# Sigmoid attention followed by a GELU MLP on one core: another order of the first loads and of TensorE's work at the start, and a last output tile in three pieces with merged stores

## The chip, the cores and the metric

The kernel runs on one core of a Trainium2 chip. The metric is the device time of one execution in microseconds (us). The kernel before takes 391.43 us (median of 3 runs, 391.25 to 391.61).

## The reference, cut to what matters

```python
# q, k, v: batch 8, heads 12, S = 448, head size 64
scores = matmul(q, k.T) / sqrt(64) - log(S)
attn   = 1 / (1 + exp(-scores))                # sigmoid, no row sums
x      = matmul(attn, v), heads side by side   # 3584 x 768
h      = x @ w_in                              # 768 x 2048
g      = 0.5 * h * (1 + tanh(c * (h + 0.044715 * h**3)))   # GELU
out    = g @ w_out                             # 2048 x 768, float32
```

## The kernel before: the parts that the change and the argument touch

The program is made by a small scheduler in Python. It simulates the engines with estimated durations, picks the next operation for each engine, and then writes out one fixed order for each. On the chip every engine follows its order and waits on semaphores; if the first operation in line has to wait, everything behind it waits too (1.23 us of TensorE in the run warm_late below).

Four heads form a *group* (3 groups per batch, 24 in all). A group has 7 score tiles ("units"). Each unit needs q and k cast to bfloat16 and transposed; four matmuls give scores of 128x896; ScalarE turns them into attention weights; four *av* matmuls add them to x transposed (xT). In the first batch (units 0 to 20) ScalarE uses Sigmoid; later batches use Tanh, and VectorE finishes the work. Tanh lies in the same table set as GELU: the profile has only two table loads, at 2.32 and 26.81 us, and after the second Tanh and GELU alternate. The MLP's first product (`make_a`, w_in) needs a complete xT of a batch; the second (`make_b`, w_out) gives tiles of 128 rows.

```python
# first group: two column ranges of q and of k, one DMA each
CUTS = ((0, NJ // 2 + 1), (NJ // 2 + 1, NJ))
for x, (lo, hi) in enumerate(CUTS):
    ld[(0, x)] = plan.add(Op("ld%s0.%d" % (nm, x),
        "AQ" if (nm, x) in (("q", 0), ("k", 1)) else "SP",     # ScalarE's or SyncE's queue
        lambda e, ...: e.dma_start(d[:, :, lo * D:hi * D], ap[:, :, lo * D:hi * D]), ...))
# ... cut ...
# the GELU table, after the last sigmoid has ended
if n == SIG * NG * NJ - 1:
    plan.add(Op("warm2", "ACT", lambda e: e.activation(warm[:], warm[:], AF.Gelu_apprx_tanh), [tanh[n]], ...))
# ... cut ...
# one output tile: two halves of 384 columns; rows of two strips, 64 partitions each
def make_b(t_, half, t):
    # ... 16 matmuls of 128x384 into one PSUM bank, copy to ob ...
    if half == 1 or last:
        for x in range(2):
            b, j = two[x]
            dst = out[b * S:(b + 1) * S, lo:hi].rearrange("(r j) d -> r j d", j=NJ)[:, j, :]
            def fn(e, x=x, dst=dst):
                return e.dma_start(dst, ob[o][64 * x:64 * x + 64, lo:hi])   # 64 rows per DMA
            if last and half == 1 and x == 1:
                at_end.append((fn, ev))                # the very last one on ScalarE's queue
                continue
            sts.append(plan.add(Op("st%d.%d" % (t_, x), "SP", fn, ...)))
# ... cut ...
# TensorE's choice before the MLP may start (not mlp)
if can and left <= 1 and free_pairs(t) and banks >= (2 if av_open else 4):
    return make_qk(n, t)                   # next score tile
if m and not soon:
    return av_take(1, t)[0]                # next av
if trans_ready(t) and banks >= (1 if soon or not 0 < n < UB else 3):
    return make_trans(t)                   # transposes of a coming group
nxt = part_ready(t)                        # two matmuls of the MLP's first product, early
return make_part(*nxt, t) if nxt and (nxt[1] or banks >= HBANKS) else None
```

## Time and profile before

| what | number | view |
|---|---|---|
| TensorE in the chain of waits | 92% of the span of 390.2 us | chain |
| first / last sigmoid starts | 7.97 / 24.89 us | timeline of ScalarE |
| xT of the first batch complete | 27.64 us | timeline of VectorE |
| first matmul of the second product | 62.03 us | timeline of TensorE |
| last copy ends; last store lands | 387.35; 389.75 us | timeline, landings |

Of the page: the first line is the span, the second the busy time of each engine with its share, the third the chain of work that ended last, by engine. In the lines below, L726 and L764 are the MLP's two products, L592 the scores, L639 the av.

```profile
span 390.2 us, 7414 instructions
PE 382.1 (98%) x3173; PEld 200.1 (51%) x3173; DVE 134.1 (34%) x229; ACT 241.9 (62%) x380; POOL 50.1 (13%) x82
PE 92%; DMA 3%; POOL 2%; ACT 1%; issue 0%
```

TensorE bounds the kernel from about 30 us to the end. Only the two ends can be shortened without taking work away. The timeline of ScalarE at the start (start us, duration us, engine, line, operation, tiles, count):

```profile
7.97 17.83 ACT L603 ACTIVATE at<-ps 128x896 bf16<-128x896 f32 x21 [0.89 <-PE ps L592]
25.87 0.92 ACT L611 ACTIVATE th<-ps 128x896 f32<-128x896 f32 x1
26.81 1.28 ACT L607 ACT_TABLE_LOAD   x1
```

The 21 sigmoids are 20 steps of 0.797 us at best (15.94 us); from first to last start they took 16.92 us, so 0.97 us was lost in gaps. TensorE's timeline shows how: at 10.07 the transposes of k and of q stand together between two score tiles (L592). At the end of the batch the last av (26.07) stands behind one more score tile (25.86).

```profile
9.75 0.38 PE L592 MATMUL ps<-qT,kT 64*64 64x448 bf16 x4
10.07 0.56 PE L546 MATMUL ps<-ident,kb 128*128 128x128 bf16 x7
10.47 0.56 PE L546 MATMUL ps<-ident,qb 128*128 128x128 bf16 x7
10.95 0.38 PE L592 MATMUL ps<-qT,kT 64*64 64x448 bf16 x4
...
25.86 0.38 PE L592 MATMUL ps<-qT,kT 64*64 64x448 bf16 x4
26.07 0.36 PE L639 MATMUL ps<-at,vb 64*64 64x448 bf16 x4
```

The end: the copies of the last tile's halves, and the DMA issue on ScalarE's queue, in the timeline.

```profile
384.26 0.49 ACT L351 ACTIVATE ob<-ps 128x384 f32<-128x384 f32 x1 [2.11 <-PE ps L764]
386.86 0.49 ACT L351 ACTIVATE ob<-ps 128x384 f32<-128x384 f32 x1 [2.11 <-PE ps L764]
387.38 0.55 ACTq L798 DMA_DIRECT2D out_dram<-ob  x1
```

The DMA issues (count, KB each, median us from issue to landing): the last tile's four stores of 64 rows land in 2.1 to 2.4 us.

```profile
out_dram<-ob SPq DMA_DIRECT2D x3, 96.0 KB, 2.1
out_dram<-ob ACTq DMA_DIRECT2D x1, 96.0 KB, 2.4
```

### The profile page before, as it was taken

The numbers are of one execution on the slowest core, as the hardware profiler recorded it, in microseconds if no ns is written. First come the engines' busy times: TensorE is split into PE (matmuls) and PEld (weight loads), VectorE is DVE, ScalarE is ACT, GpSimd is POOL, SyncE is SP. The second block draws the span as 40 slices with busy tenths as digits, with TensorE's granted clock in tenths as the row PEclk, the third lists the DMA queues.
The fourth block names the chain that finished last, engine by engine and source line by source line (L and its number), as shares of the span: only waits on it lengthen the run. The fifth ranks groups of instructions, "written<-read, shape, count | busy, mean of one in ns | idle before, by whom it ended". The sixth has DMA issues, their size and how long they took to land.

```text
span 390.2 us, 7414 instructions
## 1 busy us (share of the span) xinstructions
PE 382.1 (98%) x3173; PEld 200.1 (51%) x3173; DVE 134.1 (34%) x229; ACT 241.9 (62%) x380; POOL 50.1 (13%) x82
## 2 busy tenths in 40 slices
PE   7889999999999999999999999999999999999996
PEld 4334445545554555555555555555454555555563
DVE  3347622146634547154334423444333200000000
ACT  4999963488768888577665757575757532333221
POOL 5992110011101101110110101110000000000000
PEclk9999999999999999999999999999999999999999
DMA  8999999847984969666657818747111011111133
GB/s 229 192 195 203 210 202 306 148 113 124 284 155 126 208 159 186 164 131 176 144 121 165 179 29 183 181 69 186 40 43 42 0 42 40 42 40 42 40 81 82
DMA packets 64033, 51.74 MB, mean 133 GB/s; under 512 B 36224, under 2 KB 60544, under 8 KB 64000
## 3 DMA queue, kind: packets, MB, share of 16 engines
q1 hardware_dynamic: 48576, 36.61, 39.0%
q0 software_dynamic: 14528, 13.64, 22.2%
q10 hardware_dynamic: 896, 1.02, 0.7%
q8 instruction: 25, 0.41, 0.4%
q14 instruction: 8, 0.07, 0.1%
HBM read 45.61 MB, written 11.01 MB: 145 GB/s over the span
## 4 chain that ended last, share of the span: by engine, by line
PE 92%; DMA 3%; POOL 2%; ACT 1%; issue 0%
PE ps L726 38%; PE ps L764 38%; PE ps L592 9%; PE ps L639 7%; DMA w_in<-in_moe_w_in_dram 2%; DMA kf<-in_k_dram 1%; POOL vb L478 1%; POOL vb L480 1%; PE ps L549 1%; POOL w_in L819 0%; ACT th L611 0%; POOL qb L450 0%; POOL kb L450 0%; ACT L607 0%; PE ps L702 0%
## 5 line engine op out<-in xcount | busy, mean ns | idle before, releaser
L726 PE MATMUL ps<-xT,w_in 128*128 128x448 bf16 x756 | 153.2, 353 | 0.0
L764 PE MATMUL ps<-w_out,gT 128*128 128x384 bf16 x896 | 153.1, 326 | 0.0
L615 DVE TENSOR_SCALAR at<-th 128x896 bf16<-128x896 f32 x147 | 91.7, 628 | 134.2 <-ACT th L611 134.0
L611 ACT ACTIVATE th<-ps 128x896 f32<-128x896 f32 x147 | 129.9, 930 | 0.7 <-PE ps L592 0.7
L764 PEld LDWEIGHTS ps<-w_out,gT 128*128 128x128 bf16 x896 | 86.6, 98 | 62.5 <-issue 2.9
L726 PEld LDWEIGHTS ps<-xT,w_in 128*128 128x128 bf16 x756 | 70.5, 98 | 74.9 <-issue 7.7
L740 ACT ACTIVATE gT<-ps 128x448 bf16<-128x448 f32 x128 | 71.2, 557 | 41.8 <-PE ps L726 41.7
L351 ACT ACTIVATE ob<-ps 128x384 f32<-128x384 f32 x56 | 27.5, 490 | 95.5 <-PE ps L764 95.5
L592 PE MATMUL ps<-qT,kT 64*64 64x448 bf16 x672 | 49.4, 360 | 2.3 <-ACT at L603 1.9
L478 POOL DMA_DIRECT2D vb<-in_v_dram x24 | 14.6, 608 | 211.9 <-PE ps L592 208.3
L639 PE MATMUL ps<-at,vb 64*64 64x448 bf16 x672 | 38.3, 350 | 0.0
L592 PEld LDWEIGHTS ps<-qT,kT 64*64 64x64 bf16 x672 | 15.2, 105 | 29.2 <-issue 14.5
L639 PEld LDWEIGHTS ps<-at,vb 64*64 64x64 bf16 x672 | 19.6, 107 | 11.4 <-issue 0.7
L352 DVE CAST xT<-ps 128x448 bf16<-128x448 f32 x26 | 15.8, 618 | 13.4 <-PE ps L639 13.4
L352 DVE CAST kb<-kf 128x896 bf16<-128x896 f32 (+2 forms) x21 | 12.7, 607 | 17.7 <-DMA kf<-in_k_dram 17.6
L603 ACT ACTIVATE at<-ps 128x896 bf16<-128x896 f32 x21 | 17.5, 934 | 1.2 <-PE ps L592 0.9
L480 POOL DMA_DIRECT2D vb<-in_v_dram x24 | 16.8, 699 | 0.2 <-issue 0.2
L352 DVE CAST qb<-qf 128x896 bf16<-128x896 f32 (+1 forms) x20 | 12.3, 614 | 10.8 <-DMA qf<-in_q_dram 10.8
L351 ACT ACTIVATE xT<-ps 128x448 bf16<-128x448 f32 x22 | 12.2, 563 | 1.9 <-PE ps L639 1.9
L819 POOL DMA_DIRECT2D w_in<-in_moe_w_in_dram x16 | 9.9, 655 | 0.0
L405 PE MATMUL ps<-gT,ident 128*128 128x256 bf16 x25 | 5.7, 392 | 2.0 <-POOL ident L359 1.5
L405 PEld LDWEIGHTS ps<-gT,ident 128*128 128x128 bf16 x25 | 3.3, 141 | 3.4 <-POOL ident L359 1.5
(29 smaller groups left out, 38.7 us busy)
## 6 DMA issues: line engine op xcount, KB each, us to landing
out_dram<-ob SPq DMA_DIRECT2D x54, 192.0 KB, 2.7
kf<-in_k_dram SPq DMA_DIRECT2D x19, 448.0 KB, 3.9
qf<-in_q_dram SPq DMA_DIRECT2D x18, 448.0 KB, 5.7
vb<-in_v_dram POOLq DMA_DIRECT2D x48, 112.0 KB, 5.8
w_in<-in_moe_w_in_dram POOLq DMA_DIRECT2D x16, 192.0 KB, 11.2
w_out<-in_moe_w_out_dram POOLq DMA_DIRECT2D x4, 768.0 KB, 23.1
kb<-in_k_dram POOLq DMA_DIRECT2D x4, 224.0 KB, 8.9
qb<-in_q_dram POOLq DMA_DIRECT2D x4, 224.0 KB, 9.6
```

The costliest lines, as they stand in the source:

```text
L351: return e.activation(o, i, AF.Copy)
L352: return e.tensor_copy(o, i)
L478: a = plan.add(Op("ldv%da" % g, "SWQ", lambda e, d=dst[0:64], ap=lo: e.dma_start(d, ap), deps, 610.0, 0.0, prio=order_v(g), sem="ldv%da" % ...
L480: c = plan.add(Op("ldv%db" % g, "SWQ", lambda e, d=dst[64:128], ap=hi: e.dma_start(d, ap), deps, 610.0, 0.0, prio=order_v(g), sem="ldv%db" ...
L592: r = mm(ps[64 * half:64 * half + 64, (x, y)[a], 0:S], kv[d, a, j, :], qv[d, a, :, :], start=True, stop=True)
L603: lambda e: e.activation(at[as_][:], both, AF.Sigmoid, bias=bias, scale=scale),
L611: lambda e: e.activation(th[ts][:], both, AF.Tanh, bias=0.5 * bias, scale=0.5 * scale),
L615: lambda e: e.tensor_scalar(at[as_][:], th[ts][:], 0.5, 0.5, op0=ALU.mult, op1=ALU.add),
L639: r = mm(ps[64 * c:64 * c + 64, banks[a], 0:S], vb[s][d, slot, j, :], at[as_][d, a, :], start=(j == 0), stop=(j == NJ - 1))
L726: r = mm(ps[:, bank, 0:S], w_in[:, kt, fc * 128:(fc + 1) * 128], xT[xb][:, kt, :], start=(kt == 0), stop=(kt == KT - 1))
L740: lambda e: e.activation(gT[:, fc, col:col + S], ps[:, bank, 0:S], AF.Gelu_apprx_tanh),
L764: r = mm(ps[:, bank, 0:EH], gT[:, fc, col:col + 128], w_out[:, fc, half * EH:(half + 1) * EH], start=(fc == 0), stop=(fc == FC - 1))
```

## The change

The intent: have the first scores earlier (q's second part over both load queues), keep ScalarE's sigmoids free of gaps (no transpose close to the next score tile, scores of the second batch held until xT is complete), load the GELU table right behind the sigmoids, and make the last copy and store short (three pieces of 384, 256 and 128 columns). The core of the diff:

```diff
+    QLATE = 1
+    HOLD = 200.0
@@ first loads: q's second part as two DMAs, one on each queue; k's second part moves to SyncE's queue
-                        ld[(0, x)] = plan.add(Op("ld%s0.%d" % (nm, x), "AQ" if (nm, x) in (("q", 0), ("k", 1)) else "SP", ...
+                        both = [plan.add(Op("ld%s0.%d.%d" % (nm, x, c), eng, ... d[:, c:c + w, lo * D:hi * D] ...))
+                                for (eng, c, w) in ((("SP", 0, 1), ("AQ", 1, 1)) if (nm, x) == ("q", 1) else
+                                                    (("AQ" if nm == "q" else "SP", 0, 2),))]
+                        ld[(0, x)] = All(both)
@@ GELU table
-                    plan.add(Op("warm2", "ACT", ..., [tanh[n]], 1500.0, 1500.0))
+                    other.append(plan.add(Op("warm2", "ACT", ..., [op], 1500.0, 1500.0, prio=(1, n))))
...                                       # and each tanh waits for `other` in the plan
@@ last tile
+        def pieces(t_):
+            if t_ < NT - 1:
+                return [(0, EH), (EH, DM)]
+            return [(0, EH), (EH, DM - 128), (DM - 128, DM)]
...
+                if last and not end:
+                    b, j = two[0]
+                    dst = out[b * S:(b + 1) * S, lo:hi].rearrange("(r j) d -> j r d", j=NJ)[j:j + 2]
+                    sts.append(plan.add(Op("st%d" % t_, "SP", lambda e: e.dma_start(dst, ob[o][:, lo:hi]), [ev], ...
+                    return op
@@ TensorE's choice before the MLP
-                if can and left <= 1 and free_pairs(t) and banks >= (2 if av_open else 4):
+                if can and left <= 1 and (n < UB + 2 - QLATE or (0, KT - 1) in evac) and free_pairs(t) and ...
-                if m and not soon:
+                if m and not soon and (state["av"] < NG or m == NJ):
                     return av_take(1, t)[0]
+                ends = [tanh[x].end for x in range(max(0, n - 4), n) if ... tanh[x].end > t]
+                if 0 < n < UB and can and ends and min(ends) < t + HOLD:
+                    return None
-                return make_part(*nxt, t) if nxt and (nxt[1] or banks >= HBANKS) else None
+                return make_part(*nxt, t) if nxt and (nxt[1] or banks >= (HBANKS if n <= UB + 1 - QLATE else 1)) else None
```

The first two pieces of the last tile: their two stores of 64 rows have become one DMA of 128 rows, `j r d`.

More of the change, by code (lines that the diff above doesn't have):

```diff
@@ L417, in bass_sigmoid_attention__then__act_gelu_tanh_kernel @@
         trans = []
+        other = []
         EARLY = ("v0 q2 v1 v2 q3 v3 w0 w1 q4 v4 w2 q5 v5 w3 o0 o1 o2 o3").split()
@@ L455, in load_qk @@
                     for x, (lo, hi) in enumerate(CUTS):
-                        ld[(0, x)] = plan.add(Op("ld%s0.%d" % (nm, x), "AQ" if (nm, x) in (("q", 0), ("k", 1)) else "SP",
-                                                 lambda e, ap=ap, d=dst[0], lo=lo, hi=hi: e.dma_start(
-                                                     d[:, :, lo * D:hi * D], ap[:, :, lo * D:hi * D]),
-                                                 [], 460.0, 0.0, prio=(2, x - 2),
-                                                 sem="ld%s0.%d" % (nm, x), pkt=(16, 89.0 * (hi - lo) / NJ)))
+                        both = [plan.add(Op("ld%s0.%d.%d" % (nm, x, c), eng,
+                                            lambda e, ap=ap, d=dst[0], lo=lo, hi=hi, c=c: e.dma_start(
+                                                d[:, c:c + w, lo * D:hi * D], ap[:, c:c + w, lo * D:hi * D]),
+                                            [], 490.0, 0.0, prio=(2, -3 if x == 0 else -2 if nm == "q" else -1),
+                                            sem="ld%s0.%d.%d" % (nm, x, c), pkt=(8 * w, 89.0 * (hi - lo) / NJ)))
+                                for (eng, c, w) in ((("SP", 0, 1), ("AQ", 1, 1)) if (nm, x) == ("q", 1) else
+                                                    (("AQ" if nm == "q" else "SP", 0, 2),))]
+                        ld[(0, x)] = All(both)
                     ld[g] = ld[(0, 1)]
@@ L474, in load_v @@
             dst = vb[s][:].rearrange("p s j d -> p s (j d)")
-            deps = later(av, g - NVB) + ([ld_k[(0, 0)]] if g == 0 else [])
+            deps = later(av, g - NVB) + (ld_k[(0, 0)].ops if g == 0 else [])
             if g >= PE_TR * NG:
@@ L606, in make_qk @@
                 if n == SIG * NG * NJ - 1:
-                    plan.add(Op("warm2", "ACT", lambda e: e.activation(warm[:], warm[:], AF.Gelu_apprx_tanh),
-                                [tanh[n]], 1500.0, 1500.0))
+                    other.append(plan.add(Op("warm2", "ACT",
+                                             lambda e: e.activation(warm[:], warm[:], AF.Gelu_apprx_tanh),
+                                             [op], 1500.0, 1500.0, prio=(1, n))))
             else:
@@ L612, in make_qk @@
                                                              bias=0.5 * bias, scale=0.5 * scale),
-                                      [op, aff.get(n - NTH)], 2 * S / 1.2 + 60, 2 * S / 1.2 + 210, prio=(1, n)))
+                                      [op, aff.get(n - NTH)] + other, 2 * S / 1.2 + 60, 2 * S / 1.2 + 210, prio=(1, n)))
                 aff[n] = plan.add(Op("aff%d" % n, "DVE",
@@ L753, in bass_sigmoid_attention__then__act_gelu_tanh_kernel, with make_b @@
         store = {}
-        def make_b(t_, half, t):
+        def pieces(t_):
+            if t_ < NT - 1:
+                return [(0, EH), (EH, DM)]
+            return [(0, EH), (EH, DM - 128), (DM - 128, DM)]
+        def make_b(t_, x, t):
             bank = take(t)
@@ L759, in make_b @@
             col = (2 * t_ * 64) % (2 * S)
+            lo, hi = pieces(t_)[x]
             def fn(e):
@@ L763, in fn @@
                 for fc in range(FC):
-                    r = mm(ps[:, bank, 0:EH], gT[:, fc, col:col + 128],
-                           w_out[:, fc, half * EH:(half + 1) * EH],
+                    r = mm(ps[:, bank, 0:hi - lo], gT[:, fc, col:col + 128], w_out[:, fc, lo:hi],
                            start=(fc == 0), stop=(fc == FC - 1))
@@ L770, in make_b @@
             if t_ < 8:
-                for x in w_out_ld.values():
-                    deps += x
-            op = Op("b%d.%d" % (t_, half), "PE", fn, deps, FC * (EH / 2.4 + 2.5), 165.0, mode=128)
+                for ops in w_out_ld.values():
+                    deps += ops
+            op = Op("b%d.%d" % (t_, x), "PE", fn, deps, FC * ((hi - lo) / 2.4 + 2.5), 165.0, mode=128)
             o = t_ % NOUT
@@ L778, in make_b @@
             last = t_ == NT - 1
-            alts = copy_alts(EH)
-            if last and half == 1:
+            end = last and hi == DM
+            alts = copy_alts(hi - lo)
+            if end:
                 del alts["DVE"]
-            ev = plan.add(Op("evo%d.%d" % (t_, half), "ANY",
-                             lambda e, who: copy(e, ob[o][:, half * EH:(half + 1) * EH], ps[:, bank, 0:EH], who),
+            ev = plan.add(Op("evo%d.%d" % (t_, x), "ANY",
+                             lambda e, who: copy(e, ob[o][:, lo:hi], ps[:, bank, 0:hi - lo], who),
                              edeps, 0, 0, prio=(0, -1), alts=alts))
             give(bank, ev)
-            ev_o[(t_, half)] = ev
+            ev_o[(t_, x)] = ev
             for (b, j) in two:
@@ L789, in make_b, with fn @@
                     b_last[b] = op
-            if half == 1 or last:
+            if hi == DM or last:
                 sts = store.setdefault(t_, [])
-                lo, hi = (half * EH, half * EH + EH) if last else (0, DM)
-                for x in range(2):
-                    b, j = two[x]
-                    dst = out[b * S:(b + 1) * S, lo:hi].rearrange("(r j) d -> r j d", j=NJ)[:, j, :]
-                    def fn(e, x=x, dst=dst):
-                        return e.dma_start(dst, ob[o][64 * x:64 * x + 64, lo:hi])
-                    if last and half == 1 and x == 1:
+                left = lo if last else 0
+                if last and not end:
+                    b, j = two[0]
+                    dst = out[b * S:(b + 1) * S, lo:hi].rearrange("(r j) d -> j r d", j=NJ)[j:j + 2]
+                    sts.append(plan.add(Op("st%d" % t_, "SP", lambda e: e.dma_start(dst, ob[o][:, lo:hi]), [ev], 500.0, 0.0,
+                                           prio=(0, t_), sem="st%d.0.%d" % (o, x), pkt=(8, 145.0))))
+                    return op
+                for y in range(2):
+                    b, j = two[y]
+                    dst = out[b * S:(b + 1) * S, left:hi].rearrange("(r j) d -> r j d", j=NJ)[:, j, :]
+                    def fn(e, y=y, dst=dst):
+                        return e.dma_start(dst, ob[o][64 * y:64 * y + 64, left:hi])
+                    if end and y == 1:
                         at_end.append((fn, ev))
                         continue
-                    sts.append(plan.add(Op("st%d.%d" % (t_, x), "SP", fn,
+                    sts.append(plan.add(Op("st%d.%d" % (t_, y), "SP", fn,
                                            [ev] if last else [ev_o[(t_, 0)], ev_o[(t_, 1)]], 500.0, 0.0,
-                                           prio=(0, t_), sem="st%d.%d.%d" % (o, x, half if last else 0), pkt=(4, 145.0))))
+                                           prio=(0, t_), sem="st%d.%d.%d" % (o, y, x if last else 0), pkt=(4, 145.0))))
             return op
@@ L929, in pe_next @@
             if not mlp:
-                if can and left <= 1 and free_pairs(t) and banks >= (2 if av_open else 4):
+                if can and left <= 1 and (n < UB + 2 - QLATE or (0, KT - 1) in evac) and free_pairs(t) and banks >= (2 if av_open else 4):
                     op = make_qk(n, t)
@@ L934, in pe_next @@
                 soon = trans_ready(t) and trans[0][0] <= units[min(n + 3, len(units) - 1)][0]
-                if m and not soon:
+                if m and not soon and (state["av"] < NG or m == NJ):
                     return av_take(1, t)[0]
+                ends = [tanh[x].end for x in range(max(0, n - 4), n) if tanh[x].end is not None and tanh[x].end > t]
+                if 0 < n < UB and can and ends and min(ends) < t + HOLD:
+                    return None
                 if trans_ready(t) and banks >= (1 if soon or not 0 < n < UB else 3):
@@ L971, in pe_next @@
             op = make_b(state["b"], state["h"], t)
-            if state["h"] == 1:
+            if state["h"] == len(pieces(state["b"])) - 1:
                 for (b, j) in strips[2 * state["b"]:2 * state["b"] + 2]:
@@ L978, in pe_next @@
             else:
-                state["h"] = 1
+                state["h"] += 1
             return op
```

## The prediction

> **What bounds the kernel.** From 29.8 us on TensorE is never idle: the chain of waits gives it 92% of the 390.2 us span (38% for each MLP product). That is a fixed amount of matmul work. What counts is when TensorE fills up, how much is done by then, and the tail.
>
> Start, from the instruction timeline: q's two parts land at 5.13 and 5.88 us; the first score matmul starts at 7.54, the first sigmoid at 7.97. Then ScalarE is the limit: 21 sigmoids start every 0.797 us, except that five instructions, the last of them a tanh, come late by 0.21, 0.27, 0.27, 0.17 and 0.19 us, because transposes or MLP parts hold up the next scores. The last sigmoid starts at 24.89; the last av comes behind one more score tile at 26.07; the two xT copies end at 27.64. Only then does the MLP run freely. From 24 to 29.8 us TensorE lost about 0.8 us idle and 0.8 us in eight changes of array mode (0.29 from an av to an MLP part against 0.19 without). The Trainium skill ("TensorEngine Tiling (Array Packing)", Key Properties) says a mode change drains the array; this agrees.
>
> Tail: last matmul starts at 386.50, its 384-column copy runs 386.86 to 387.35, two 96 KB stores issued at 387.37 land at 389.51 and 389.75.
>
> **The change.**
> 1. q's second part over both queues: 704 instead of nearly 896 KB must land before it. It lands about 0.4 us earlier, but TensorE transposes the first part until 6.24, so only a warm-up matmul and a short wait go: first sigmoid 0.2 us earlier.
> 2. No transpose close to the next score tile: removes most of the first four stalls, 0.7 to 0.9 us.
> 3. Score tiles after n=21 wait for xT: the last av follows its sigmoid at once, 0.2 us. Together xT is complete 1.2 us earlier (26.4).
> 4. GELU table behind the last sigmoid: the load swaps place with one tanh; about 0. The Trainium skill ("ScalarE: Activation LUTs", What ACT_TABLE_LOAD costs) gives 1283 ns plus a drain of 1380 ns; the trace shows 1.283 us and only 0.017 us idle before it: no drain to win.
> 5. The first w_in slice still lands at 23.85 us, limited by its queue. Before that TensorE lacks MLP work, so not all of the 1.2 us is kept: I estimate 1.0 (one more score and av tile before 23.9, 0.4; idle and mode changes, 0.6).
> 6. Last tile: 384-column matmuls start every 162.5 ns; 256 and 128 columns should take 109 and 57 ns (transposes of 128 columns ran at 57), +0.05 us in all. The last copy falls from 0.49 to about 0.28, the last stores from 96 to 32 KB; 192 KB landed in 2.6 us and 96 KB in 2.1 to 2.4, which extrapolates to 0.3 less. Tail: 0.5 us.
>
> **Sum.** 391.43 - 1.0 - 0.5 = 389.9 us, range 389.1 to 390.8. Chances: faster by over 2% 0.01, within 2% 0.98, slower 0.01.
>
> **Right if:** first sigmoid near 7.8; no ScalarE gap within the sigmoids; table load behind them near 24.7; both xT copies done near 26.4; first second-product matmul near 61.2 instead of 62.2; tail shorter by 0.4 to 0.5 us.
>
> **Wrong if:** holding TensorE only moves its idle time past 24 us; the new order after 26 us has more mode changes or waits for PSUM banks; ScalarE, 93% busy from 40 to 50 us, becomes the limit because its tanhs start later; the middle store (128 KB) delays the last ones.

## More of the kernel before

A profile has its own span, about 1.8 us shorter than the time that belongs to it; spans are compared with spans only.

The windows view over the end (stretch, then length and busy time of PE, PEld, DVE, ACT, POOL; then TensorE's clock, the mean busy share of the 16 DMA engines, GB/s):

```profile
384.00:386.00 2.00, 2.00 (x14) 1.17 (x12) 0.00 (x0) 0.49 (x1) 0.00 (x0) 1.00 0.46 130
386.00:388.00 2.00, 0.82 (x6) 0.29 (x3) 0.00 (x0) 0.49 (x1) 0.00 (x0) 1.00 0.40 88
388.00:390.00 2.00, 0.00 (x0) 0.00 (x0) 0.00 (x0) 0.00 (x0) 0.00 (x0) 0.88 0.37 98
```

## The result, and the profile after

The changed kernel takes 395.61 us (median of 6 runs, 395.35 to 397.36) against 391.48. The ratio is 1.0113, with a 95% interval of 1.0095 to 1.0131. Here and below a ratio is the mean time of one kernel's fast runs over the mean of the other's in the same rounds, so it is not quite the ratio of the quoted medians. The forecast was 389.9, range 389.1 to 390.8. The time lies outside: the change costs 4.1 us where 1.5 us were to be won.

```profile
span 393.5 us, 7448 instructions
PE 381.8 (97%) x3189; PEld 201.2 (51%) x3189; DVE 134.4 (34%) x230; ACT 241.0 (61%) x380; POOL 51.1 (13%) x82
PE 94%; ACT 3%; POOL 0%; issue 0%; POOLq 0%
```

The chain does not lead to the cause: the view of the DMA issues ties no landing to the two merged stores. One has to look at the ends oneself. The start looks as forecast. ScalarE's timeline: 21 sigmoids, 16.21 us from the first to the last start (16.92 before), and the table load directly behind.

```profile
7.50 17.12 ACT L609 ACTIVATE at<-ps 128x896 bf16<-128x896 f32 x21 [0.69 <-PE ps L598]
24.64 1.28 ACT L614 ACT_TABLE_LOAD   x1
...
26.04 0.90 ACT L618 ACTIVATE th<-ps 128x896 f32<-128x896 f32 x1
27.44 0.92 ACT L618 ACTIVATE th<-ps 128x896 f32<-128x896 f32 x1 [0.50 <-PE ps L598]
```

TensorE's timeline shows something at the end of the batch that I had not foreseen: not a score tile but an early MLP part (L709) now stands in front of the last av (L646).

```profile
24.25 0.36 PE L646 MATMUL ps<-at,vb 64*64 64x448 bf16 x4
24.54 0.55 PE L709 MATMUL ps<-xT,w_in 128*128 128x448 bf16 x2
25.02 0.38 PE L646 MATMUL ps<-at,vb 64*64 64x448 bf16 x4
```

The first matmul of the second product starts at 60.74 us (62.03 before), and the last copy of all ends at 385.88 (387.35 before): TensorE is 1.3 us earlier in these two profiles. So all of the loss, and more, comes after the last copy. The end in the timeline:

```profile
382.96 0.49 ACT L353 ACTIVATE ob<-ps 128x384 f32<-128x384 f32 x1 [2.11 <-PE ps L778]
383.48 2.18 SPq L810 DMA_DIRECT2D out_dram<-ob  x2
384.71 0.38 ACT L353 ACTIVATE ob<-ps 128x256 f32<-128x256 f32 x1 [1.26 <-PE ps L778]
385.60 0.28 ACT L353 ACTIVATE ob<-ps 128x128 f32<-128x128 f32 x1 [0.51 <-PE ps L778]
385.91 0.50 SPq L818 DMA_DIRECT2D out_dram<-ob  x1
385.91 0.54 ACTq L818 DMA_DIRECT2D out_dram<-ob  x1
```

Everything there is as forecast: a last copy of 0.28 us, stores issued at once. But the DMA issues say when the stores landed: the 32 KB of the last SyncE store took 7.1 us where 96 KB had taken 2.1.

```profile
out_dram<-ob SPq DMA_DIRECT2D x1, 32.0 KB, 7.1
out_dram<-ob ACTq DMA_DIRECT2D x1, 32.0 KB, 4.4
```

And the windows show a DMA system that is mostly empty all that time: a share of 0.10 to 0.28, where it was 0.37 to 0.46 before. The share counts packets under way, averaged over 16 engines (in full load, from 26 to 28 us, it reads 1.27); two engines with one packet each would be 0.125.

```profile
384.00:386.00 2.00, 1.57 (x23) 1.33 (x20) 0.00 (x0) 0.66 (x2) 0.00 (x0) 1.00 0.10 24
386.00:388.00 2.00, 0.00 (x0) 0.00 (x0) 0.00 (x0) 0.00 (x0) 0.00 (x0) 1.00 0.19 38
388.00:390.00 2.00, 0.00 (x0) 0.00 (x0) 0.00 (x0) 0.00 (x0) 0.00 (x0) 0.77 0.28 74
390.00:392.00 2.00, 0.00 (x0) 0.00 (x0) 0.00 (x0) 0.00 (x0) 0.00 (x0) 0.50 0.14 48
```

From the end of the last copy to the end of the span it takes 7.64 us against 2.87, so 4.77 us more; with the last copy 1.47 us earlier the span grows by 3.30 us, which is 393.52 less 390.22.

The trace's list of DMA packets gives a count. A store of 64 rows leaves 16 packets of 4 bytes besides its data; I read each as the end of one engine's share. Before, the last tile's four stores left 64 such packets, 4 times 16. After, its four stores left 36: 16 + 16 for the two 64-row stores, and 2 + 2 for the merged ones. The 1 KB packets of the middle piece came at 12 in each quarter of a microsecond and took 0.046 us each: 2.2 at a time. The semaphores of the packed trace say the same, and give the landings that the view leaves out: each merged store raised its own once before its data moved and then only twice more (389.95 and 390.00 us; 392.78 and 392.81), where a 64-row store raises it 16 times. The first store's packets ran from 384.70 to 389.67, the second's from 389.62 to 392.49, one store behind the other.

### The profile page after: what moved, and what is told of

Its sections match the earlier page's. It is cut to its first block, busy times and chain, and to the rows that moved or that the text cites. A ratio compares the mean times of both kernels' runs of the same rounds, so it can differ in the third digit from the quotient of the medians.

```text
span 393.5 us, 7448 instructions
## 1 busy us (share of the span) xinstructions
PE 381.8 (97%) x3189; PEld 201.2 (51%) x3189; DVE 134.4 (34%) x230; ACT 241.0 (61%) x380; POOL 51.1 (13%) x82
## 4 chain that ended last, share of the span: by engine, by line
PE 94%; ACT 3%; POOL 0%; issue 0%; POOLq 0%
PE ps L778 37%; PE ps L733 37%; PE ps L598 9%; PE ps L646 7%; ACT at L609 3%; PE ps L407 1%; PE ps L709 1%; PE ps L555 1%; PE ps L552 0%; POOL ident L361 0%; ACT ob L353 0%; POOL ident L360 0%; POOLq L361 0%; POOLq L1081 0%
## 5 line engine op out<-in xcount | busy, mean ns | idle before, releaser
L778 PE MATMUL ps<-w_out,gT 128*128 128x384 bf16 (+2 forms) x912 | 152.8, 323 | 0.0
L778 PEld LDWEIGHTS ps<-w_out,gT 128*128 128x128 bf16 x912 | 87.6, 98 | 61.8 <-issue 3.6
L353 ACT ACTIVATE ob<-ps 128x384 f32<-128x384 f32 (+2 forms) x57 | 27.7, 485 | 96.7 <-PE ps L778 96.7
L484 POOL DMA_DIRECT2D vb<-in_v_dram x24 | 15.0, 624 | 209.5 <-PE ps L598 206.2
L646 PE MATMUL ps<-at,vb 64*64 64x448 bf16 x672 | 38.2, 350 | 0.0
L646 PEld LDWEIGHTS ps<-at,vb 64*64 64x64 bf16 x672 | 19.5, 107 | 12.0 <-issue 0.7
L486 POOL DMA_DIRECT2D vb<-in_v_dram x24 | 17.4, 724 | 0.2 <-issue 0.2
L354 DVE COPY kT<-ps 128x896 bf16<-128x896 bf16 (+2 forms) x7 | 3.9, 553 | 3.3 <-PE ps L552 1.7
```

Source lines behind the costliest of these rows:

```text
L353: return e.activation(o, i, AF.Copy)
L354: return e.tensor_copy(o, i)
L484: a = plan.add(Op("ldv%da" % g, "SWQ", lambda e, d=dst[0:64], ap=lo: e.dma_start(d, ap), deps, 610.0, 0.0, prio=order_v(g), sem="ldv%da" % ...
L486: c = plan.add(Op("ldv%db" % g, "SWQ", lambda e, d=dst[64:128], ap=hi: e.dma_start(d, ap), deps, 610.0, 0.0, prio=order_v(g), sem="ldv%db" ...
L646: r = mm(ps[64 * c:64 * c + 64, banks[a], 0:S], vb[s][d, slot, j, :], at[as_][d, a, :], start=(j == 0), stop=(j == NJ - 1))
L778: r = mm(ps[:, bank, 0:hi - lo], gT[:, fc, col:col + 128], w_out[:, fc, lo:hi], start=(fc == 0), stop=(fc == FC - 1))
```

## The experiments

**Theory 1.** A DMA whose outermost dimension is 2 runs on 2 of the 16 DMA engines. The two merged stores need about 5 and 3 us there, and the last store, though spread over all engines, has shares on these two and waits in line. **Rival 2:** the short packets (1 KB, 512 B) or the third piece cost the time. **Rival 3:** the new order of work at the start costs it.

The Trainium skill states the rule of theory 1 in "DMA: Bandwidth & Descriptors", section "Why a DMA increments its semaphore by 16 and not by 1": of each of the two access patterns the slowest dimension that is not 1 counts, and the DMA uses the largest number of engines, up to 16, that divides both. I had not applied it to the merged store. Packet counts (2, 15, 1, below) agree with it.

### The tail

**fix_two_stores**: the changed kernel, each piece stored by two DMAs of 64 rows.

```diff
-                if last and not end:
-                    b, j = two[0]
-                    dst = ...rearrange("(r j) d -> j r d", j=NJ)[j:j + 2]
-                    sts.append(... e.dma_start(dst, ob[o][:, lo:hi]) ...)
-                    return op
```

> The changed kernel with one edit: each piece of the last tile is stored by two DMAs of 64 rows, as before, in place of one DMA whose outermost dimension is 2. Theory 1 (a DMA whose outermost dimension is 2 runs on 2 of the 16 DMA engines, so 192 KB took about 5 us and the last store queued behind it): the 7.1 us from copy end to last landing falls to about 2.2, span near 388.5, time near 389.6, 1.8 us under before. Rival 2 (the short packets of 1 KB and 512 B or the third piece cost the time): stays above 394. Rival 3 (the new order of work at the start costs it): stays above 394.

Measured: 390.87 us (median of 5) against 391.66 beside it, ratio 0.9993 (0.9980 to 1.0006). The tail after the last copy fell from 7.64 to 2.85 us, and the last two stores land as fast as before:

```profile
out_dram<-ob ACTq DMA_DIRECT2D x1, 32.0 KB, 2.0
out_dram<-ob SPq DMA_DIRECT2D x1, 32.0 KB, 1.9
```

Rivals 2 and 3 fall: the three pieces, their short packets and the new start are all still there. But the time is 1.3 us above the forecast of 389.6. That opens a second question, taken up below.

**tail_only**: the kernel before with `pieces` and the merged stores alone (that part of the diff, nothing else).

> The kernel before with nothing but the last tile's three pieces and merged stores. Theory 1 and rival 2: last copy ends 0.2 us earlier (387.15), last landing about 7 us after it, so about 4.5 us slower than before, 396.0. Rival 3: 391.4 or a little less.

Measured: 396.04 us, ratio 1.0116 (1.0103 to 1.0129); tail 7.64 us, as in the changed kernel to the hundredth. The whole loss is in this part.

**start_only**: the changed kernel with the old tail.

```diff
-            return [(0, EH), (EH, DM - 128), (DM - 128, DM)]     # and no merged store
+            return [(0, EH), (EH, DM)]
```

> The changed kernel with the old tail: two halves, each stored by two DMAs of 64 rows. Theories 1 and 2: the last copy ends 1.3 us earlier than before (386.05), the tail after it is 2.9 us as before, time about 390.15, 1.3 us faster. Rival 3: above 394.

Measured: 391.35 us, ratio 1.0013 (0.9990 to 1.0036); one of six runs was at 393.86. No loss at the start, but none of the expected 1.3 us either.

**one_merged_half**: the kernel before; only the first half's two stores merged.

```diff
+                if last and half == 0:
+                    dst = out[b * S:(b + 1) * S, lo:hi].rearrange("(r j) d -> j r d", j=NJ)[j:j + 2]
+                    sts.append(... e.dma_start(dst, ob[o][:, lo:hi]) ...)
+                    return op
```

> The kernel before, two halves, only the first half's two stores merged into one DMA with outermost dimension 2: packets stay at 1536 B, no third piece. Theory 1: 64 rows on each of two engines at about 0.078 us a row take 5 us (about 385.8 to 390.8), and the last half's store on the same queue ends behind them near 391.2 in place of 389.5: about 1.6 us slower, 393.0. Rival 2: no change, 391.4. Rival 3: no change.

Measured: 393.97 us, ratio 1.0061 (1.0045 to 1.0077): slower, by more than forecast (2.4 us of the means, not 1.6). No third piece, no packet under 1536 B. The last two stores, unchanged, landed in 4.0 and 4.3 us where they had taken 2.1 and 2.4:

```profile
out_dram<-ob SPq DMA_DIRECT2D x1, 96.0 KB, 4.0
out_dram<-ob ACTq DMA_DIRECT2D x1, 96.0 KB, 4.3
```

The very last store goes over ScalarE's queue, the merged one over SyncE's, and it is delayed as well. The Trainium skill's page named above ("DMA: Bandwidth & Descriptors") fits: in its section "Why a DMA increments its semaphore by 16 and not by 1" a DMA from these queues on fewer engines takes the lowest-numbered ones, and by "Issuing engines are not separate DMA queues" both queues run on the same sixteen. No trace here has the numbers of the engines.

**rows60, rows62, rows61**: is it the number of engines? The kernel before; SyncE's very last store of 64 rows is split into 60 + 4, 62 + 2 or 61 + 3 rows. Number of DMAs, packet size and bytes are the same in all three. By the skill's rule, told above, the first of the two runs on 15, 2 and 1 engines.

```diff
+                    if last and half == 1:
+                        for n, (r0, r1) in enumerate(((0, 62), (62, 64))):      # 60, 62 or 61
+                            sts.append(... e.dma_start(dst[r0:r1], ob[o][r0:r1, lo:hi]) ...)
+                        continue
```

> The kernel before, with only the very last 64-row store of the SyncE queue split into two DMAs of 60 and 4 rows (same packets of 1536 B). Theory 1, sharpened by what the skill states (a DMA is spread over the largest number up to 16 that divides the row count): 60 rows go over 15 engines and 4 rows over 4; one more issue of 0.5 us, so at most 0.5 us slower, 391.4 to 391.9. Rival (rows are always spread over all 16 engines): the same.

> The same with 62 and 2 rows. Theory 1: 2 engines carry 31 rows each at about 0.075 us, 2.3 us from data start at 388.4, so the last landing moves from 389.7 to about 390.8 to 391: 1.0 to 1.3 us slower than before. Rival: equal to the run with 60 rows.

> The same with 61 and 3 rows. Theory 1: 61 is prime, one engine carries 61 rows at about 0.075 us, 4.6 us, last landing near 393.0: about 3.3 us slower than before. Rival: equal to the run with 60 rows.

| rows | engines by the rule | 4-byte packets of the last three stores | tail after last copy | time | ratio to before (95%) |
|---|---|---|---|---|---|
| 60 + 4 | 15 and 4 | 35 = 16 + 15 + 4 | 2.81 us | 391.31 | 1.0000 (0.9987 to 1.0013) |
| 62 + 2 | 2 and 2 | 20 = 16 + 2 + 2 | 4.73 us | 393.40 | 1.0050 (1.0037 to 1.0063) |
| 61 + 3 | 1 and 3 | 20 = 16 + 1 + 3 | 6.70 us | 395.57 | 1.0104 (1.0091 to 1.0117) |

In the windows view from 390 to 391 us the run with 62 rows moves 35 GB/s and the run with 61 rows 25 GB/s:

```profile
390.00:391.00 1.00, 0.00 (x0) 0.00 (x0) 0.00 (x0) 0.00 (x0) 0.00 (x0) 0.50 0.10 35
```

```profile
390.00:391.00 1.00, 0.00 (x0) 0.00 (x0) 0.00 (x0) 0.00 (x0) 0.00 (x0) 1.00 0.07 25
```

Theory 1 stands. One row moved from the second store to the first, 61 + 3 for 60 + 4, changes the time by 4.3 us, and nothing else differs. My sizes were about 0.8 us low, here and in one_merged_half; I had not counted that the other queue's store has shares on the same engines, which may be why.

### Why the repaired tail is no shorter than the old one

In fix_two_stores the copy is short, yet the tail is 2.85 us, not the 2.2 or so that its small last stores suggested. SyncE's queue has five issues in a row (start 383.79, 3.38 us), and the last store leaves at 386.58 while ScalarE's, ready at the same time, left at 386.23:

```profile
383.79 3.38 SPq L812 DMA_DIRECT2D out_dram<-ob  x5
...
386.23 0.55 ACTq L812 DMA_DIRECT2D out_dram<-ob  x1
```

**mid_on_act**: as fix_two_stores, with the middle piece's second store issued from ScalarE, behind its own copy.

```diff
+                    if last and y == 1 and x == 1:
+                        at_mid.append((fn, ev))
+                        continue
...
+                    for fn, ev in at_mid:                 # while ScalarE's order is written out
+                        if op is ev:
+                            eng.wait_ge(sem["ACT"], level["ACT"][ev.target])
+                            fn(eng).then_inc(sem["mid"], 16)
```

> The changed kernel with 64-row stores everywhere (as the run that uses two stores per piece) and the middle piece's second store issued on ScalarE's queue behind its own copy. In the two-store run SyncE's queue was still issuing the middle piece's second store until 386.52, so the last store left at 386.58 and not 386.23. Expected: last SyncE store leaves right behind the last copy, last landing 0.3 us earlier, copy later by under 0.1; span 0.25 us shorter than the two-store run, time near 390.7. If the issue order is not the limit: no change.

Measured: tail 2.55 us, 0.30 less, as expected; the copy is 0.1 us later. Time 390.97, ratio 0.9991 (0.9979 to 1.0003).

### Where the gain of the start went

The forecast was 1.0 us from the start. fix_two_stores, whose start is the changed one, should have shown most of it and did not. The profiles of all these runs help, because many share one start. Means of six profiles each (old start: before, tail_only, one_merged_half and the three with rows; new start: after, fix_two_stores, start_only and three of the mid_on_act kernel):

| us | old start (range) | new start (range) | gain | forecast |
|---|---|---|---|---|
| first sigmoid | 7.56 (7.00 to 7.97) | 7.49 (7.22 to 7.83) | 0.07 | 0.2 |
| time lost between the 21 sigmoids | 0.98 (0.80 to 1.43) | 0.46 (0.27 to 1.05) | 0.52 | 0.7 to 0.9 |
| last sigmoid starts | 24.48 | 23.89 | 0.59 | about 1.0 |
| xT complete | 27.23 | 26.91 | 0.32 | 1.2 |
| second product begins | 61.58 (60.83 to 62.03) | 61.14 (60.74 to 61.29) | 0.44 | 1.0 |

So the start wins about 0.4 us, not 1.0. (From the scatter of the six profiles I estimate 0 to 0.9 for the begin of the second product.) First, the one profile that I had read was the latest of six in its first sigmoid and in the begin of the second product. Such an execution differs in when TensorE's clock rises: in tail_only (first sigmoid at 7.00) the warm-up matmuls of 256 columns go from 213 to 110 ns a piece at 4.2 us, in the profile of before they still take 213 ns at 7 us. By the clock records of the six profiles the clock rose between 4.22 us (first sigmoid at 7.00) and 7.30 us (7.88); the three that rose by 5.7 us had it at 7.00 to 7.40, the three after 7.0 at 7.77 to 7.97. The Trainium skill ("TensorE: Matmul & The Clock Gate", "Part 1: The HAM clock gate") says that the window for this runs freely, so the moment changes from run to run; these profiles agree, and the spread that goes with it, up to 1 us at the first sigmoid, is as large as the gain sought. Second, the last av now comes 1.3 us behind the start of the last sigmoid (25.02 less 23.71), where before it was 1.2 (26.07 less 24.89): the score tile that I had counted out (step 3) was replaced by an early MLP part. Third, the loads: the gaps come back when the second group's k and q land late.

**no_qsplit, no_hold, no_qlate, warm_late**: fix_two_stores with one part of the start undone in each. These four ran together on another chip than fix_two_stores, without it as a control, and the scheduler plans anew for each. One kernel, mid_on_act, moved by 0.2% between two chips (0.9991 and 0.9972, below), so differences of that size between these runs and fix_two_stores cannot be read.

```diff
no_qsplit:  the first loads of q and k as in the kernel before
no_hold:    -    HOLD = 200.0      +    HOLD = 0.0
no_qlate:   -    QLATE = 1         +    QLATE = -1000      # scores not held, old bank rule for parts
warm_late:  -    [op], 1500.0, 1500.0, prio=(1, n)   +    [tanh[n]], 1500.0, 1500.0    # and no `+ other`
```

> The two-store run's kernel with q's and k's first loads as in the kernel before. So far first sigmoids were at 7.00 to 7.97 us in six profiles with the old loads and at 7.22 to 7.83 in four with the new, and k's second part landed at 5.7 to 6.2 (old) against 6.5 to 8.0 (new), where the late ones stopped ScalarE for 0.3 to 0.5 us. Theory S (the split wins at most 0.2 us for the first scores and gives it back through k): k's second part lands before 6.3, no stall at the fifth sigmoid, time equal to the two-store run within 0.3 us, 391.1. Rival (my prediction's step 1): 0.2 us slower than the two-store run, steadily.

Measured: 391.20, ratio 0.9987 (0.9974 to 0.9999). k's second part landed at 5.79, the first sigmoid was at 7.22. Step 1 of the prediction finds no support: the split wins nothing that shows in the time.

> The two-store run's kernel without the hold before the next score tile. Theory: the three stalls of 0.21, 0.27 and 0.27 us at the transposes come back in place of 0.14 and 0.08, so 21 sigmoids take 0.5 us longer. If the end of the sigmoids sets the time: 0.5 us slower than the two-store run. If the landing of the first w_in slice (22.5 to 23.9 us, whatever the order of work) sets it: under 0.2 us slower.

Measured: 391.54, ratio 0.9997 (0.9985 to 1.0009). The gaps of 0.25 and 0.26 us are back in its profile, so the hold does what it is for. The time differs from the two-store run's by less than the intervals resolve.

> The two-store run's kernel without holding score tiles after n=21 until xT is complete, and without the freer bank rule for early MLP parts. Theory: the 0.50 us gap of ScalarE behind the first tanh goes, the last av comes 0.2 us later; MLP start within 0.2 us of the two-store run, time within 0.3 us.

Measured: 391.79, ratio 1.0009 (0.9995 to 1.0023): the slowest of the four by its mean, and more than I had expected, but its interval overlaps that of no_hold and of fix_two_stores. xT is complete at 26.51, but the second product begins only 34.75 us later, where fix_two_stores takes 34.11. TensorE stands still where an early part waits for an xT copy that ScalarE could start only at 25.98 (to 26.51), behind the table load (24.58 to 25.87) and the small GELU that calls for it, while VectorE's copy of the other half had started at 25.59:

```profile
25.47 0.55 PE L709 MATMUL ps<-xT,w_in 128*128 128x448 bf16 x2
26.65 1.29 PE L709 MATMUL ps<-xT,w_in 128*128 128x448 bf16 x6 [0.63 <-ACT xT L353]
```

> The two-store run's kernel with the GELU table load where the kernel before has it, one tanh later. Theory (my step 4): the load moves 0.93 us back behind one tanh and nothing else follows: time within 0.2 us.

Measured: 390.95, ratio 0.9989 (0.9976 to 1.0003). Moving the table load is worth nothing that shows, as step 4 said. Its profile caught a bad start: k of the second group landed at 10.09 us, and TensorE stood 1.2 us in front of the transposes that stand before the fifth score tile in its order.

```profile
9.57 0.28 PE L407 MATMUL ps<-gT,ident 128*128 128x256 bf16 x1
11.09 0.56 PE L552 MATMUL ps<-ident,kb 128*128 128x128 bf16 x7 [1.23 <-DVE kb L354]
```

Two candidates were left for what eats the rest of the gain: **K**, the landing of the second group's k and q (the later of the two lands between 8.3 and 10.1 us in these profiles; with both there by 8.9 us the changed starts lost 0.27 to 0.40 us between their sigmoids; at 8.93 mid_on_act lost 0.65 and v_later 1.01; with the later one at 9.9 to 10.1 us no_qsplit, no_hold and warm_late lost 1.23, 1.64 and 1.57); **W**, the landing of the first w_in slice (22.5 to 23.9 us), for which an early MLP part waits in front of the last avs.

**w_in_sooner**: mid_on_act with another order on GpSimd's queue alone; the order on every other engine is the same. **v_later**: w_in_sooner, and GpSimd's queue starts when k's second part has landed. **mid_again**: their control.

```diff
-        EARLY = ("v0 q2 v1 v2 q3 v3 w0 w1 q4 v4 w2 q5 v5 w3 o0 o1 o2 o3").split()
+        EARLY = ("v0 q2 v1 v2 q3 w0 w1 v3 q4 v4 w2 q5 v5 w3 o0 o1 o2 o3").split()
v_later, besides:
-            deps = later(av, g - NVB) + (ld_k[(0, 0)].ops if g == 0 else [])
+            deps = later(av, g - NVB) + (ld_k[(0, 1)].ops if g == 0 else [])
```

> The same kernel as the run with the middle store on ScalarE's queue, as the control of the two others on their chip: first landing of both loads of the second head group between 8.8 and 10.1 us, a sigmoid stall of 0.1 us if by 8.9 and about 0.1 us more for each 0.1 us later; tail 2.55 us; time 390.9.

Measured: 390.37, ratio 0.9972 (0.9960 to 0.9985).

> As the control, only the GpSimd queue's order changed: the fourth head group's v after the first two w_in slices; order of work on all compute engines the same. Theory W (the part of the MLP that stands in TensorE's order before the last avs waits for w_in in some executions, and this eats the start's gain): the first slice lands about 1.1 us earlier (near 22.2), TensorE never waits for it, 0.1 to 0.3 us faster than the control. Theory K (what eats the gain is the late landing of the second head group's k and q): equal to the control.

Measured: 390.58, ratio 0.9974 (0.9960 to 0.9987). The slice landed at 22.43 instead of 23.64, and the time did not move. W falls as a cause that shows in the mean.

> As w_in_sooner, and the GpSimd queue starts only when k's second part has landed (6.5 to 8 us) in place of its first (4.5), so that the loads of the first two head groups have the DMA engines to themselves. Theory K: both second-group loads land by 8.5, no stall over 0.15 us at the fifth to ninth sigmoid, 0.3 us faster than w_in_sooner unless v's first load (then near 11) holds the first av. Theory W: everything on the GpSimd queue 1.7 us later, the first w_in slice near 23.9, TensorE waits for it, 0.3 us or more slower.

Measured: 391.70, ratio 1.0000 (0.9987 to 1.0012), so 1.1 us slower than its control. The remedy did not work: k landed at 8.93 all the same, and the sigmoids still lost 0.78 us at the fifth. It does not decide for or against K, but its trace says more of what K is: the two casts on VectorE run one after the other. q landed at 8.72 and was cast from 8.75, so k's cast began only at 9.42, and TensorE waited 0.67 us for it; in w_in_sooner, with k at 8.87 but q at 7.59, k's cast began at 8.93 and nothing was lost at the fifth. Why v_later is slower was not tested by itself: everything on GpSimd's queue came later (v at 10.75, w_in at 24.51), and the scheduler also gave TensorE another order, from its 78th matmul on.

**trans_later**: mid_on_act, with the second group's transposes one score tile later in TensorE's order. **mid_third**: its control.

```diff
+            if trans[0][0] == 1 and state["n"] < 5:
+                return False
```

> The kernel with the middle store on ScalarE's queue, and the second head group's transposes placed one score tile later in TensorE's fixed order (behind the fifth tile, not the fourth). Theory K (TensorE stands in front of these transposes whenever k and q of the second group, and their casts, are later than about 8.9 us): a stall of more than 0.3 us at the fifth sigmoid disappears even if both loads land as late as 9.6; time 0.2 to 0.4 us under the control on average, because only the late executions gain. If the landing is not what stops the sigmoids: equal to the control.

Measured: 390.76, ratio 0.9982 (0.9968 to 0.9995).

> The control of trans_later on the same chip: 0.1 to 0.4 percent faster than before, as in its two earlier runs (390.97 and 390.37); sigmoid stall by the landing of the second group: 0.15 us if by 8.9, 1 us if near 10.

Measured: 390.25, ratio 0.9973 (0.9960 to 0.9985). trans_later is not faster than its control. Its profile fell in an execution with early loads (8.58 us), so the case it was made for is not in a profile. K is seen in single profiles (warm_late above all) but not shown to set the mean; how much of the missing 0.6 us it takes stays open.

**A version that beats both.** The mid_on_act kernel, the change with 64-row stores and one store moved to ScalarE's queue, was 0.9991, 0.9972 and 0.9973 of the kernel before in three groups of runs; the last two intervals lie below 1. It is the simplest of the best versions here (w_in_sooner at 0.9974 cannot be told from it): 0.1 to 0.3% under the kernel before, where the change itself is 1.1% above it.

## Why the prediction was wrong

- **What bounds the kernel: right.** TensorE is the chain before and after, and only the ends moved.
- **Step 6, the tail: wrong, and this is the step that failed.** It reckoned stores by their bytes ("the last stores from 96 to 32 KB; ... extrapolates to 0.3 less") and named the merged middle store only as a risk that might delay the last ones. The last store took 7.07 us, not 1.8: the merged DMAs ran on 2 engines of 16. Instead of 0.5 us won, the tail after the last copy lost 4.77. The copy itself was sized right (0.28 us), and so were the matmuls.
- **Even without that, step 6 was too hopeful**: with 64-row stores the tail after the copy stayed at 2.85 us (2.87 before), because the additional issues on SyncE's queue let the last store leave 0.35 us late. With that put right (mid_on_act) the tail is 2.55 us, 0.32 less than before: the 0.3 us that step 6 had estimated for smaller stores holds once they run on all engines and leave at once.
- **Step 1, the split of q: wrong in effect.** q's second part did land earlier (5.48 against 5.88; in the mean of six profiles 5.46 against 5.66), but the first sigmoid moved by 0.07 us in the mean of six profiles, and undoing it cost no time that shows.
- **Step 2, the hold: right mechanism, size too large.** The sigmoids lost 0.46 us in place of 0.98: 0.52 won, where 0.7 to 0.9 were forecast.
- **Step 3: wrong in mechanism; its worth is open.** The last av does not follow its sigmoid at once, because an MLP part took the score tile's place. Whether holding the scores is worth anything is not shown: no_qlate was the slowest of the four, but the intervals overlap.
- **Step 4: right**, about 0.
- **Step 5, the sum of the start: 1.0 forecast, 0.44 measured** (mean begin of the second product). The base was one profile, and that profile was the latest of its six at this point. Of the 5.7 us by which the forecast missed, this step is some 0.6; the rest is step 6.

## What to carry to other kernels

Before merging two DMAs, look at the outermost dimension on both sides: 64 rows twice used all 16 engines, one DMA of 2 x 64 rows used two, and a row count of 61 or 62 in place of 64 or 60 cost 2 to 4 us. A transfer that is spread well still ends with its slowest share, so a badly spread DMA also delays what is issued after it, on the other queue too. And where a change is worth tenths of a microsecond at the start of a kernel, read several profiles of the kernel before: one alone can be off by as much as the gain.

## What the Trainium skill lacked or had wrong

- "DMA: Bandwidth & Descriptors", "Rules for kernel authors", advises against two transfers to disjoint partition halves and for one 128-partition transfer. Here that merge made the tail 4.79 us longer (7.64 against 2.85 us in fix_two_stores, which differs in nothing else), because the DRAM side's outermost dimension became 2. The same table has the caution, in its row "Use all 16 engines", but the row on partition halves does not point to it.
- The same page has the rule for the number of engines right (15, 2 and 1 engines for 60, 62 and 61 rows, by the count of 4-byte packets). I found no figure there for what a narrow DMA does to later ones: 32 KB, itself on 16 engines, landed 7.07 us after its issue, where the same store in mid_on_act took 1.79 us (386.55 to 388.34).
- "ScalarE: Activation LUTs", "What ACT_TABLE_LOAD costs", counts about 2.66 us for a switch, 1.28 of load and 1.38 of drain. The load agrees (1.28 us); from the end of the last sigmoid to the next tanh the changed kernel's ScalarE lost 1.42 us in all (24.62 to 26.04), with no drain to be seen.
- "TensorE: Matmul & The Clock Gate" calls the ramp's penalty under 1% and not worth fitting. That holds (1 us of 390), but it was as large as the gain sought at the start: first sigmoids from 7.00 to 7.97 us in six profiles with one order of work, with the clock's rise between 4.22 and 7.30 us.
